# ScalarE writes the band's mask into the score banks, and the score products accumulate onto it

## The chip, the core and the metric

The kernel runs on one core of one Trainium2 chip. The metric is the device time of one execution in microseconds (us). The core's engines work side by side, each through its own list of instructions in a fixed order: TensorE (PE) multiplies matrices, VectorE (DVE) and ScalarE (ACT) work element by element, GpSimd (POOL) does too but cannot reach the accumulator banks, and SyncE (SP) issues the transfers. An instruction that needs another engine's result waits for a semaphore, and everything behind it on its engine waits with it.

## The reference, cut to what matters

```python
# B, H, S, D = 8, 8, 576, 64; factor = 4; scale = 1/8
out_d = softmax(scale * mean4(q) @ mean4(k).T) @ mean4(v)      # pooled attention, repeated 4 times
mask = abs(pos[:, None] - pos[None, :]) < factor               # a band 7 wide
scores = where(mask, scale * q @ k.T, -1e9)
s = scores - max(scores); a = exp(s); a /= sum(a) + 1e-9
x = (repeat(out_d, 4) + a @ v) -> [4608 tokens, 512]
h = x @ w_in                                                    # 512 -> 2048
out = (h * clip(h + 3, 0, 6) / 6) @ w_out                       # 2048 -> 512
```

## The kernel before

**The two halves.** The attention makes x, and two large products (the MLP) use it. The MLP's products are done as three 128x512 matmuls each (high and low parts), so PE has 2,688 wide matmuls of 512 columns for seven chunks of 512 tokens (lines 1066 and 1125; a chunk is 384 of them), and a last pair of chunks in Strassen's form (lines 1380, 1481, 1634). A chunk's first products (L1066) read x in split parts ("rounded"), so they can start only when the attention of the batches in it is done: L754 adds the two attentions into x, a cast and a subtraction split it (L122, L987).

**A unit** is one batch and one pair of heads. Batches 0 and 1 are worked on alone. The 24 units of batches 2 to 7 (called unit 0 to 23 here) go through PE in *bursts*: one burst holds the score products of a new unit, pooled (L504) and banded (L706), and between them the products with v (L749, L667) of the unit two bursts earlier. So x of batch 2 (units 0 to 3) is complete after the sixth burst, that of unit 5. A burst needs the banks h0 and h1, which the MLP uses too, and the banks a0 and a1 for its scores: columns 0 to 319 of each hold five windows of the band, 64 by 64, and the next 144 the pooled scores.

**After a burst, before the change.** DVE adds the mask to the banded scores of either bank while it copies them to SBUF (`outside`, L722), then takes the maximum of all ten windows (L557); ACT makes ten exponentials from SBUF with their sums (L568). ACT also makes the pooled softmax (L544, L550, L554: called a *weigh* here, three per unit, two of them from the banks), the mean (L687) and four copies out of the h banks (L122). A bank is given back when its `outside` and its weigh are done.

**What sets the order.** A planner in the kernel places every operation on its engine with a cost in us, due times, buffers ("take" and "free") and a table of shifts by operation number. What it writes out is the fixed order of each engine; on the chip only semaphores hold an instruction back. The score banks are taken in the units' order.

Of the kernel before, what the change touches and what calls it, by code (L numbers as in the profile page):

```python
# [58 lines left out]
def tile_local_down_attention_moe(ctx, tc, q_all, k_all, v_all, _qk_loc, _v_loc, w_in, w_out, ident_d, _mask_d, out):  # L59
# [67 lines left out]
    hot = const.tile([P, P], BF16, name="hot")  # L127
    mask = const.tile([P, D], F32, name="mask")
    head = const.tile([NAR, 2], F32, name="head")
# [14 lines left out]
    def make_mask():  # L144

        z = scratch()
        for h in range(2):
            hs = slice(h * D, (h + 1) * D)
            nc.vector.tensor_copy(z[hs, HALO:HALO + D], ident[hs, hs])
        near = bass.AP(tensor=z.tensor, offset=z.offset, ap=[z.ap[0], [1, D], [1, W]])  # L150
        nc.vector.tensor_reduce(out=mask, in_=near, op=ALU.add, axis=AX.X)
        nc.vector.tensor_scalar(mask, mask, -1.0, -MASKED, op0=ALU.add, op1=ALU.mult)

# [85 lines left out]
    loads = []  # L239
# [127 lines left out]
    def plan_unit(b, d, u, row0, k0, kv, PS, pair, masked, early_user, due):  # L367
# [120 lines left out]
        def scores_d4(hb):  # L488

            if not mixed:  # L490
                for g in range(2):
                    st["ps", g] = bank(PS, ("s", un, g))
# [4 lines left out]
            for h, j in ((0, 0), (1, 1), (0, 2), (1, 0), (0, 1), (1, 2)):  # L497
# [3 lines left out]
                for i in range(halves):  # L501
# [3 lines left out]
                        ps, q4[hs, j * QSTEP:j * QSTEP + QS], k4[hs, ks], start=True, stop=True, skip_group_check=True)  # L505
# [193 lines left out]
        def scores():  # L699

            for jj in range(5):
                for g in range(2):
                    k_first = window(jj + 5 * g)[0]
                    for h in range(2):
# [3 lines left out]
                            qk_of("k")[hs, k_first:k_first + WIN], start=True, stop=True, skip_group_check=True)  # L708
# [102 lines left out]
        else:  # L811
            sd, hx = yield {
                "un": un, "after": turned["q"] + turned["k"] + [pooled["q"], pooled["k"]] + masked,
                "take": [sk] + bks, "free": [], "pooled": scores_d4, "banded": scores}
# [21 lines left out]
        if True:  # L836
            subs = []
            for g in range(2):
                subs.append(op("DVE", 0.4, partial(outside, g), [sl_op] + subs, take=[pl, sl], free=[bks[g]]))
# [3 lines left out]
        elif not alone:  # L843
            a = op("ACT", 0.12, lambda: nc.scalar.activation(st["m"], st["m"], AF.Copy, scale=-0.125), [a])
# [856 lines left out]
    spare = const.tile([1, 2], F32, name="spare")  # L1701
# [559 lines left out]
```

## Time and profile before

| | |
|---|---|
| three runs | 882.73 us median (879.83 to 883.11) |
| span of the profiled execution | 877.6 us; no time around it is given for this execution |
| PE busy in the span | 871.4 us (99%) |
| DVE, ACT, POOL busy | 662.0 (75%), 494.0 (56%), 266.6 us (30%) |
| granted TensorE clock, mean | 0.999 |

The span goes from the first to the last instruction. Busy PE time counts overlapping matmuls once, so short waits between two matmuls can hide in it; how many wide matmuls pass in a stretch tells more.

### The profile page before, as it was taken

What the parts mean: (1) busy time and instruction counts of PE and PEld (TensorE: products, weight loads), DVE (VectorE), ACT (ScalarE), POOL (GpSimd) and SP (SyncE); (2) the same over time, 40 slices, a digit from 0 to 9 for tenths busy, and PEclk for the clock granted to TensorE, in tenths of its full rate; (3) what the DMA queues carried; (4) which work ended last, traced back from release to release, by engine and by line L of the source; (5) the groups of instructions that cost most, each with busy time, mean ns of one, the idle gap of its engine ahead of it and who ended that gap; (6) DMA issues with size and microseconds to landing.
All of it is one profiled execution on the core that took longest, in us unless ns stands there. A gap on an engine that the chain in (4) does not pass through costs nothing.

```text
span 877.6 us, 19793 instructions
## 1 busy us (share of the span) xinstructions
PE 871.4 (99%) x6948; PEld 716.1 (82%) x6948; DVE 662.0 (75%) x1240; ACT 494.0 (56%) x1555; POOL 266.6 (30%) x384
## 2 busy tenths in 40 slices
PE   8999999999999999999999999999999999999998
PEld 6788788888888888888888888888888888888887
DVE  7998886556867687877866786667856768778984
ACT  5998765455663656455454555555552325557761
POOL 6657742132524243224323431333422110000000
PEclk9999999999999999999999999999999999999999
DMA  9999353555675677757465647677764117564894
GB/s 255 262 294 234 74 129 79 118 102 123 121 164 120 120 149 165 148 128 148 98 156 122 141 102 167 146 174 234 188 151 103 37 38 230 212 228 137 274 274 71
DMA packets 358735, 136.40 MB, mean 155 GB/s; under 512 B 269612, under 2 KB 331180, under 8 KB 358636
## 3 DMA queue, kind: packets, MB, share of 16 engines
q1 hardware_dynamic: 353052, 134.22, 62.1%
q10 hardware_dynamic: 5584, 0.92, 0.6%
q8 instruction: 55, 0.90, 0.4%
q14 instruction: 44, 0.36, 0.1%
HBM read 90.44 MB, written 44.63 MB: 154 GB/s over the span
## 4 chain that ended last, share of the span: by engine, by line
PE 98%; DMA 1%; DVE 1%; SPq 0%; issue 0%
PE o L1125 36%; PE h L1066 35%; PE h L1380 5%; PE o L1634 4%; PE a L1380 4%; PE a L1634 2%; PE o L1481 2%; PE a L706 2%; PE h L749 2%; PE a L504 1%; PE h L667 1%; PE o L339 1%; DMA rows<-in_q_dram 1%; PE a L594 0%; PE a L684 0%; PE h L504 0%
## 5 line engine op out<-in xcount | busy, mean ns | idle before, releaser
L1125 PE MATMUL o<-wp,rounded 128*128 128x512 f32 x1344 | 323.6, 392 | 0.0
L1066 PE MATMUL h<-rounded,wp 128*128 128x512 f32 x1344 | 316.3, 390 | 0.0
L1066 PEld LDWEIGHTS h<-rounded,wp 128*128 128x128 f32 x1344 | 251.4, 188 | 52.8 <-DVE rounded L987 0.2
L1125 PEld LDWEIGHTS o<-wp,rounded 128*128 128x128 f32 x1344 | 249.6, 188 | 53.2 <-issue 0.4
L1076 DVE SCALAR_TENSOR_TENSOR arena<-arena,h 128x512 f32<-128x512 f32 x112 | 75.7, 676 | 52.7 <-ACT arena L1072 52.2
L1072 ACT ACTIVATE arena<-h 128x512 f32<-128x512 f32 x112 | 66.5, 594 | 84.8 <-PE h L1066 83.7
L1080 ACT CAST rounded<-arena 128x512 fp32r<-128x512 f32 x112 | 69.0, 616 | 62.9 <-PE o L1125 37.4
L1084 DVE TENSOR_TENSOR rounded<-arena,rounded 128x512 fp32r<-128x512 f32 x79 | 61.1, 774 | 51.7 <-PE o L1125 42.3
L568 ACT ACTIVATE arena<-arena 128x64 f32<-128x64 f32 x240 | 80.2, 337 | 0.4
L1084 POOL TENSOR_TENSOR rounded<-arena,rounded 128x512 fp32r<-128x512 f32 x33 | 44.8, 1359 | 94.3 <-PE o L1125 60.0
L1188 POOL TENSOR_TENSOR arena<-arena 128x128 f32<-128x128 f32 x65 | 33.1, 509 | 52.9 <-DVE arena L1183 28.0
L390 DVE STREAM_TRANSPOSE arena<-arena 128x576 f32<-128x576 f32 x56 | 43.0, 769 | 6.5 <-DMA arena<-in_k_dram 3.6
L544 ACT ACTIVATE arena<-arena 128x1 f32<-128x1 f32 (+1 forms) x77 | 15.0, 195 | 55.7 <-DVE arena L557 55.7
L568 ACT ACTIVATION_READ_ACCUMULATOR arena<-arena 128x1 f32 x240 | 45.3, 189 | 0.0
L687 ACT ACTIVATE arena<-h 128x144 f32<-128x144 f32 x24 | 7.0, 291 | 64.5 <-PE h L667 64.5
L447 POOL TENSOR_TENSOR arena<-arena 32x256 f32<-32x256 f32 (+2 forms) x28 | 21.2, 756 | 58.4 <-DMA arena<-in_v_dram 58.3
L1380 PE MATMUL h<-wp,wp 128*128 128x512 f32 x144 | 35.4, 389 | 0.0
L445 DVE TENSOR_REDUCE arena<-arena 128x128 f32<-128x512 f32 (+2 forms) x28 | 29.8, 1066 | 6.6 <-PE h L667 4.4
L585 DVE TENSOR_TENSOR arena<-arena 128x640 f32<-128x640 f32 (+1 forms) x40 | 32.9, 824 | 1.1
L1380 PEld LDWEIGHTS h<-wp,wp 128*128 128x128 f32 x144 | 27.0, 188 | 5.6
L557 DVE TENSOR_REDUCE arena<-arena 128x10 f32<-128x640 f32 (+1 forms) x57 | 31.4, 556 | 0.1
L1183 POOL TENSOR_TENSOR arena<-wp 128x256 f32<-128x256 f32 x21 | 17.0, 817 | 43.9 <-DMA si<-arena 18.1
(273 smaller groups left out, 1371.0 us busy)
## 6 DMA issues: line engine op xcount, KB each, us to landing
rawp<-in_w_in_dram SPq DMA_DIRECT2D x16, 512.0 KB
rawp<-in_w_out_dram SPq DMA_DIRECT2D x16, 512.0 KB
arena<-in_q_dram SPq DMA_DIRECT2D x112, 72.0 KB
arena<-in_k_dram SPq DMA_DIRECT2D x112, 72.0 KB
pl<-arena SPq DMA_DIRECT2D x24, 320.0 KB
arena<-pl SPq DMA_DIRECT2D x96, 80.0 KB
arena<-in_v_dram SPq DMA_DIRECT2D x28, 256.0 KB
wd<-wp SPq DMA_DIRECT2D x12, 512.0 KB
```

Source lines behind the costliest of these rows:

```text
L390: nc.vector.transpose(out=qk[kind], in_=qk[kind])
L568: nc.scalar.activation(x[:, j], x[:, j], AF.Exp, bias=m[:, j:j + 1], scale=0.125, accum_out=s[:, j:j + 1])
L585: eng.tensor_tensor(x, x, s.unsqueeze(2).broadcast_to(list(x.shape)), op=ALU.mult)
L1066: nc.tensor.matmul(st["ps"], win[f][:, wt, kk * P:(kk + 1) * P], xs[part][:, kk], start=(kk == 0 and i == 0), stop=(kk == NK - 1 and i == ...
L1072: nc.scalar.activation(st["t"], st["ps"], AF.Relu, bias=3.0)
L1076: nc.vector.scalar_tensor_tensor(out=t, in0=t, scalar=6.0, in1=st["ps"], op0=ALU.min, op1=ALU.mult)
L1080: nc.scalar.copy(st["gh"], st["t"])
L1084: eng.tensor_tensor(st["gl"], st["t"], st["gh"].bitcast(F32), op=ALU.subtract)
L1125: nc.tensor.matmul(otile[n, m], gt[:, ms], wout[f][:, wt], start=(f == 0 and i == 0), stop=(f == NF - 1 and i == 2),)
L1188: eng.tensor_tensor(u[:, z], u[:, x], u[:, y], op=o)
L1380: nc.tensor.matmul(ps, weight(i, j, wt, kk), xpart(MOVING[j], part)[:, kk], start=first and kk == 0 and x == 0, stop=kk == half - 1 and x ...
L1634: nc.tensor.matmul(places[acc, m][:, ts], w, z[:, part, ts], start=j == 5 and i == 0 and x == 0, stop=i == NG - 1 and x == 2, skip_group_c ...
```

## The change

From batch 2 on, ACT first copies a tile `seeds` (five copies of the mask, then zeros for the pooled part; 464 columns) into both score banks (`seed`). The burst's score products no longer start afresh but accumulate onto it. DVE's add is gone: it takes the maximum of each bank (`top_rows`), and the ten exponentials read the banks and write SBUF. The banks are given back when those ten are done. Once, two matmuls over the whole banks (`fill_bank`) come first, and POOL makes `seeds`.

```diff
+    def fill_bank():
+        for g in range(2):
+            ps = bank("a", ("open", g))
+            nc.tensor.matmul(ps, hot, hot.unsqueeze(1).broadcast_to([P, 4, P]), start=True, stop=True, skip_group_check=True)
+    def make_seeds(eng):
+        eng.tensor_copy(seeds[:, D:5 * D].rearrange("p (j k) -> p j k", k=D), mask.unsqueeze(1).broadcast_to([P, 4, D]))
+        eng.memset(seeds[:, 5 * D:], 0.0)
...
-                        ps, q4[hs, j * QSTEP:j * QSTEP + QS], k4[hs, ks], start=True, stop=True, skip_group_check=True)
+                        ps, q4[hs, j * QSTEP:j * QSTEP + QS], k4[hs, ks], start=n == 2 or mixed, stop=True, skip_group_check=True)
...
-                    x[:, j], x[:, j], AF.Exp, bias=m[:, j:j + 1], scale=0.125, accum_out=s[:, j:j + 1])
+                    x[:, j], rows(j % 2)[:, j // 2], AF.Exp, bias=m[:, j:j + 1], scale=0.125, accum_out=s[:, j:j + 1])
...
-                            qk_of("k")[hs, k_first:k_first + WIN], start=True, stop=True, skip_group_check=True)
+                            qk_of("k")[hs, k_first:k_first + WIN], start=alone, stop=True, skip_group_check=True)
+        def seed(g):
+            st["ps", g] = ps = bank(PS, ("s", un, g))
+            nc.scalar.copy(ps[:, :5 * D + SD], seeds)
+        def top_rows(g):
+            if g == 0:
+                places()
+            top(rows(g), greatest(g))
...
+            filled = [op("ACT", 0.49, partial(seed, g), opened, take=[bks[g]]) for g in range(2)]
             sd, hx = yield {
-                "un": un, "after": turned["q"] + turned["k"] + [pooled["q"], pooled["k"]] + masked,
-                "take": [sk] + bks, "free": [], "pooled": scores_d4, "banded": scores}
+                "un": un, "after": turned["q"] + turned["k"] + [pooled["q"], pooled["k"]] + filled,
+                "take": [sk], "free": [], "pooled": scores_d4, "banded": scores}
...
-                subs.append(op("DVE", 0.4, partial(outside, g), [sl_op] + subs, take=[pl, sl], free=[bks[g]]))
-            a = op("DVE", 0.73, lambda: top(p_all(), st["m"]), subs)
+            subs.append(op("DVE", 0.4, partial(outside if alone else top_rows, g), [sl_op] + subs, take=[pl, sl], free=[bks[g]]))
...
-                a = op("ACT", 0.67, lambda j=j: exps_sums(j, p_all(), st["m"], st["s"]), [m, a])
+                a = op("ACT", 0.67, lambda j=j: exps_sums(j, p_all(), st["m"], st["s"]), [m, a], free=bks)
```

The planner then writes another order. All engines' orders are the same up to the middle of the chunk of batch 0; from there they differ in many places. PE's content is unchanged but for the two matmuls of `fill_bank`. In the rows below the first number is the place in the engine's order, and the line numbers of the changed kernel are some 10 to 21 higher: L575 is the exponential (L568 before), L720 the seed, L1037 the eviction of a result (L1016), L694 the mean (L687), L697 and L771 the combination and the addition into x (L690, L754), L1087 and L1146 the MLP's products (L1066, L1125).

ACT before, between the bursts of unit 4 and unit 5 (`a_2708` is a score bank of unit 4, `h_2924` an h bank of unit 5's burst):

```order
305 L550 ACTIVATE arena<-a_2708,arena 128x144
306 L554 ACTIVATE arena<-arena 128x1
307 L568 ACTIVATE arena<-arena 128x64 x2
308 L1072 ACTIVATE arena<-h_2801 128x512
309 L568 ACTIVATE arena<-arena 128x64 x2
310 L122 CAST rounded<-arena 128x2x128
```

Row 305 is the last that reads unit 4's banks; the exponentials behind it read SBUF, and unit 5's burst needs no ACT instruction after row 305 for its score banks.

ACT with the change, the same stretch (`a_2718`, `a_2724` are unit 4's score banks, `a_2958`, `a_2962` unit 5's):

```order
355 L561 ACTIVATE arena<-arena 128x1
356 L575 ACTIVATE arena<-a_2718,arena 128x64
357 L575 ACTIVATE arena<-a_2724,arena 128x64
358 L1037 ACTIVATE arena<-o_2015 128x512
359 L575 ACTIVATE arena<-a_2718,arena 128x64
360 L575 ACTIVATE arena<-a_2724,arena 128x64
361 L575 ACTIVATE arena<-a_2718,arena 128x64
362 L575 ACTIVATE arena<-a_2724,arena 128x64
363 L575 ACTIVATE arena<-a_2718,arena 128x64
364 L575 ACTIVATE arena<-a_2724,arena 128x64
365 L582 ACTIVATE arena<-arena 128x10
366 L720 COPY a_2958<-seeds 128x464
```

Ten exponentials of unit 4 (two stand ahead, rows 351 and 352) and an eviction now stand ahead of unit 5's seeds, of which row 367 is the second.

PE before, at the end of unit 5's burst and the start of the third chunk (`h_3042` is that chunk's first product):

```order
556 L706 MATMUL a_2926<-arena 64x64 x2
557 L706 MATMUL a_2927<-arena 64x64 x2
558 L1125 MATMUL o_2000<-wp_1715,rounded 128x512 x3
559 L1125 MATMUL o_2005<-wp_1715,rounded 128x512 x3
560 L1125 MATMUL o_2013<-wp_1715,rounded 128x512 x3
561 L1125 MATMUL o_2023<-wp_1715,rounded 128x512 x3
562 L1125 MATMUL o_2000<-wp_1750,rounded 128x512 x3
563 L1125 MATMUL o_2005<-wp_1750,rounded 128x512 x3
564 L1066 MATMUL h_3042<-rounded,wp_557 128x512 x12
```

Eighteen wide matmuls of the chunk before stand between the burst and the third chunk; between unit 4's burst and this one stand 60.

PE with the change, the same place:

```order
540 L1146 MATMUL o_2035<-wp_1775,rounded 128x512 x3
541 L511 MATMUL a_2958<-arena 64x144 x2
542 L511 MATMUL a_2962<-arena 64x144 x2
```

```order
566 L713 MATMUL a_2958<-arena 64x64 x2
567 L713 MATMUL a_2962<-arena 64x64 x2
568 L1087 MATMUL h_3053<-rounded,wp_555 128x512 x6
569 L1087 MATMUL h_3067<-rounded,wp_630 128x512 x6
570 L1087 MATMUL h_3053<-rounded,wp_555 128x512 x6
571 L1087 MATMUL h_3067<-rounded,wp_630 128x512 x6
572 L1087 MATMUL h_3114<-rounded,wp_745 128x512 x12
573 L1087 MATMUL h_3142<-rounded,wp_756 128x512 x12
```

Row 540 is the last product of the second chunk: unit 5's burst has moved behind all of it, 36 wide matmuls after unit 4's, and the third chunk's first product stands right behind the burst.

DVE with the change, behind unit 5's burst (`h_2965` is its h bank):

```order
323 L564 TENSOR_REDUCE arena<-a_2958 128x1
324 L564 TENSOR_REDUCE arena<-a_2962 128x1
325 L697 SCALAR_TENSOR_TENSOR arena<-h_2965,arena 128x144
326 L400 STREAM_TRANSPOSE arena<-arena 128x576
327 L771 TENSOR_TENSOR first<-h_2964,arena 128x288
328 L771 TENSOR_TENSOR first<-h_2965,arena 128x288
```

Two maxima and a transposition of a later unit stand around the combination, ahead of the two additions that complete batch 2's x.

## Rows read from the trace of the kernel before

**Rows 1.** The page, busy time: engine, us, share, instructions.

```profile
PE 871.4 (99%) x6948; PEld 716.1 (82%) x6948; DVE 662.0 (75%) x1240; ACT 494.0 (56%) x1555; POOL 266.6 (30%) x384
```

**Rows 2.** Stretches: length, busy us (instructions) of each engine, granted clock, DMA share, GB/s.

```profile
core 0: us, PE busy (x) PEld busy (x) DVE busy (x) ACT busy (x) POOL busy (x), PEclk, DMA share, GB/s
34.00:690.00 656.00, 656.00 (x5596) 540.39 (x5600) 486.44 (x938) 373.50 (x1316) 236.51 (x336) 1.00 0.63 144
874.00:876.00 2.00, 0.00 (x0) 0.00 (x0) 0.34 (x1) 0.00 (x0) 0.00 (x0) 0.98 0.73 102
876.00:877.60 1.60, 0.00 (x0) 0.00 (x0) 0.00 (x0) 0.00 (x0) 0.00 (x0) 0.50 0.17 24
```

**Rows 3.** Timeline around unit 5's burst: start us, us, engine, line, operation, count.

```profile
231.81 0.48 PE L504 MATMUL a<-arena 64*64 64x144 f32 x8
...
233.52 0.29 ACT L687 ACTIVATE arena<-h 128x144 f32<-128x144 f32 x1 [2.17 <-PE h L667]
...
233.99 4.38 PE L1125 MATMUL o<-wp,rounded 128*128 128x512 f32 x18
...
234.63 0.31 DVE L690 SCALAR_TENSOR_TENSOR arena<-h,arena 128x144 f32<-128x144 f32 x1 [0.37 <-ACT arena L122]
...
235.06 0.81 DVE L754 TENSOR_TENSOR first<-h,arena 128x288 f32<-128x288 f32 x2
...
236.07 0.50 ACT L122 CAST rounded<-first 128x384 fp32r<-128x384 f32 x1
...
236.64 1.01 POOL L987 TENSOR_TENSOR rounded<-first,rounded 128x384 fp32r<-128x384 f32 x1 [5.21 <-ACT rounded L122]
...
238.21 4.02 PE L1066 MATMUL h<-rounded,wp 128*128 128x512 f32 x17
```

**Rows 4.** Timeline of ACT behind unit 4's burst.

```profile
217.51 0.29 ACT L687 ACTIVATE arena<-h 128x144 f32<-128x144 f32 x1 [1.21 <-PE h L667]
...
221.29 0.20 ACT L544 ACTIVATE arena<-arena 128x1 f32<-128x1 f32 x1 [2.70 <-DVE arena L557]
...
223.94 0.33 ACT L568 ACTIVATE arena<-arena 128x64 f32<-128x64 f32 x1
...
224.27 0.33 ACT L568 ACTIVATE arena<-arena 128x64 f32<-128x64 f32 x1
```

**Rows 5.** Groups of ACT by form: count, busy us, mean ns, idle before.

```profile
L568 ACT ACTIVATE arena<-arena 128x64 f32<-128x64 f32 x240 | 80.2, 337 | 0.4
...
L550 ACT ACTIVATE arena<-a,arena 128x144 f32<-128x144 f32 x48 | 18.3, 382 | 2.9 <-DVE arena L722 1.4
...
L550 ACT ACTIVATE arena<-arena 128x144 f32<-128x144 f32 x24 | 10.0, 416 | 0.8
...
L1396 ACT COPY arena<-a 128x512 f32<-128x512 f32 x12 | 7.1, 588 | 11.0 <-PE a L1380 10.8
...
L193 ACT ACTIVATE a<-rawp 128x512 f32<-128x512 f32 x2 | 1.3, 650 | 0.0
```

**Rows 6.** Groups of DVE by form.

```profile
L1076 DVE SCALAR_TENSOR_TENSOR arena<-arena,h 128x512 f32<-128x512 f32 x112 | 75.7, 676 | 52.7 <-ACT arena L1072 52.2
...
L390 DVE STREAM_TRANSPOSE arena<-arena 128x576 f32<-128x576 f32 x56 | 43.0, 769 | 6.5 <-DMA arena<-in_k_dram 3.6 <-DMA arena<-in_q_dram 2.9
L722 DVE TENSOR_TENSOR arena<-a,mask 128x320 f32<-128x320 f32 x56 | 26.7, 481 | 1.7 <-ACT arena L550 1.1 <-ACT arena L531 0.3 <-issue 0.2
...
L557 DVE TENSOR_REDUCE arena<-arena 128x10 f32<-128x640 f32 x29 | 23.5, 810 | 0.1
...
L557 DVE TENSOR_REDUCE arena<-a 128x1 f32<-128x144 f32 x56 | 15.9, 295 | 0.2 <-PE a L706 0.2
```

**Rows 7.** Timeline of PE, first and last microseconds.

```profile
1.06 3.17 PE L1695 MATMUL h<-hot 128*128 128x512 bf16 x7 [1.06 <-DVE hot L140]
4.03 1.57 PE L322 MATMUL a<-ident,arena 128*128 128x128 f32 x6
5.39 1.84 PE L322 MATMUL o<-ident,arena 128*128 128x128 f32 x12
...
873.33 0.52 PE L1634 MATMUL o<-wp,wp 128*128 128x256 f32 x3
```

More of the change, by code (lines that the diff above doesn't have):

```diff
@@ L124, in copy_on @@
             eng.tensor_copy(out_, in_)
-    hot = const.tile([P, P], BF16, name="hot")
-    mask = const.tile([P, D], F32, name="mask")
-    head = const.tile([NAR, 2], F32, name="head")
+    seeds = const.tile([P, 5 * D + SD], F32, name="seeds")
+    mask, hot = seeds[:, :D], seeds[:, 5 * D:5 * D + P // 2].bitcast(BF16)
+    small = const.tile([P, 4], F32, name="small")
+    head, spare = small[:NAR, :2], small[:1, 2:]
     def scratch():
@@ L237, in xb_of @@
         return ("xb", b) if b > 1 else ("xb1", 1) if b else ("tail", 0)
-    loads = []
+    loads, opened = [], []
     def src(t, first, ap):
@@ L488, in scores_d4 @@
         def scores_d4(hb):
-            if not mixed:
-                for g in range(2):
-                    st["ps", g] = bank(PS, ("s", un, g))
             st["hb"] = hb
@@ L811, in plan_unit @@
         else:
+            if not opened:
+                opened.append(op("PE", 0.5, fill_bank, take=[(PS, ("open", g)) for g in range(2)], free=[(PS, ("open", g)) for g in range(2)], rec=2))
+                opened.append(op("POOL", 0.6, partial(make_seeds, nc.gpsimd), opened + masked))
+            filled = [op("ACT", 0.49, partial(seed, g), opened, take=[bks[g]]) for g in range(2)]
             sd, hx = yield {
-                "un": un, "after": turned["q"] + turned["k"] + [pooled["q"], pooled["k"]] + masked,
-                "take": [sk] + bks, "free": [], "pooled": scores_d4, "banded": scores}
+                "un": un, "after": turned["q"] + turned["k"] + [pooled["q"], pooled["k"]] + filled,
+                "take": [sk], "free": [], "pooled": scores_d4, "banded": scores}
             sl_op = sd
@@ L835, in plan_unit @@
         s_ops.append(sl_op)
-        if True:
-            subs = []
-            for g in range(2):
-                subs.append(op("DVE", 0.4, partial(outside, g), [sl_op] + subs, take=[pl, sl], free=[bks[g]]))
+        subs = []
+        for g in range(2):
+            subs.append(op("DVE", 0.4, partial(outside if alone else top_rows, g), [sl_op] + subs, take=[pl, sl], free=[bks[g]]))
+        if alone:
             a = op("DVE", 0.73, lambda: top(p_all(), st["m"]), subs)
@@ L843, in plan_unit @@
         elif not alone:
-            a = op("ACT", 0.12, lambda: nc.scalar.activation(st["m"], st["m"], AF.Copy, scale=-0.125), [a])
+            a = op("ACT", 0.12, lambda: nc.scalar.activation(st["m"], st["m"], AF.Copy, scale=-0.125), subs)
             m = a
             for j in range(0, NWIN, 2):
-                a = op("ACT", 0.67, lambda j=j: exps_sums(j, p_all(), st["m"], st["s"]), [m, a])
+                a = op("ACT", 0.67, lambda j=j: exps_sums(j, p_all(), st["m"], st["s"]), [m, a], free=bks)
             a = op("ACT", 0.15, lambda: plus(st["s"]), [a])
@@ L1700, in tile_local_down_attention_moe @@
     begun = op("SP", 0.5, lambda: None, size=0.0001, dl=-9.0)
-    spare = const.tile([1, 2], F32, name="spare")
     plain = op("POOL", 0.2, lambda: nc.gpsimd.memset(spare, 0.0), dl=-2.0)
```

## The prediction

> **What bounds the kernel now.** I read the busy times first: PE is at work in 871.4 of 877.6 us [rows 1]. Then the stretches: from 34 to 690 us, where all the units of the attention pass, PE is busy for the whole 656.00 us at clock 1.00, while DVE and ACT have 170 and 282 us to spare [rows 2]. So PE's own instructions are the bound, and nothing that makes another engine quicker can shorten that stretch; a change can only leave PE's time as it is or put a wait into it. The question is therefore not what DVE saves, but whether a burst, or a chunk's first product, now has to wait with no other work left for PE. Last I read the place where that is closest before: in the timeline around unit 5's burst [rows 3] the burst starts at 231.81, the eighteen wide matmuls behind it at 233.99, and the third chunk's first product at 238.21. Batch 2's x, which that product needs, is added up at 235.06 + 0.81 = 235.87, cast and split by 237.65. The eighteen matmuls cover this with 2.3 us to spare for the addition; for the split, which only the second half of the products needs, there is more.
>
> **What the change takes away.** 48 additions of the mask of 0.48 us and 24 maxima of 0.81 us; the 48 maxima that come instead handle 320 columns each, as the addition does, so I price them at 0.48 us [rows 6]. DVE gets back 24 x 0.81 = 19 us of time that PE never waited for: worth nothing.
>
> **What it adds on PE.** Two full matmuls of `fill_bank`. The seven matmuls of the same shape at the kernel's start are 2.97 / 7 = 0.42 us apart [rows 7], at the lower of the two clock levels, so some 0.21 each at the upper one; with a change of shape, 0.5 us together. Accumulating costs PE nothing that the wide matmuls, which nearly all accumulate, don't show already.
>
> **What it adds on ACT.** 48 seeds of 464 columns. No row before shows one; the nearest are the copy out of a bank, 0.588 us for 512 columns, and an activation into a bank, 0.650 [rows 5]. In proportion that is 0.53 to 0.59, and ACT's instructions overlap by some 0.1 us: I take 1.05 us for a pair, from its start to its end. ACT is busy for 373.50 of the 656 us [rows 2], so 25 us more of it has room. But the seeds stand in the way of the burst: a burst now waits for its seeds, these for the ten exponentials of the unit before (they read the banks), and these stand behind that unit's maxima and weighs.
>
> **How long that chain is.** Before, from a burst's start to the mean it takes 233.52 - 231.81 = 1.71 us [rows 3], and from unit 4's mean to its first exponential 223.94 - 217.51 = 6.43 us [rows 4], with all three weighs between. From the first exponential on, ten of them follow 0.33 us apart [rows 4], 3.3 us. An exponential that reads a bank has no row; the weigh, in both forms, is 34 ns quicker from a bank (382 against 416 ns [rows 5]). So the ten take 3.0 to 3.3 us; I keep 3.3. With the seeds and a signal of 0.1 us the least chain is 1.71 + 6.43 + 3.3 + 1.05 + 0.1 = 12.6 us from burst to burst, plus what the order puts between.
>
> **Where it shows.** On PE's side a burst takes 2.18 us (231.81 to 233.99) and eighteen wide matmuls 4.22 [rows 3]. In the new order the 24 seeded bursts have 23 gaps. Eighteen hold 81 matmuls or more, over 21 us with the burst: the chain is hidden. Four hold 60, or 2.18 + 14.1 = 16.2 us; there the order puts two evictions and one or two small casts of the MLP into the chain, some 1.8 us, so 14.4: hidden, with 1.8 us to spare. One holds 36, unit 4 to unit 5: 2.18 + 8.4 = 10.6 us, and one eviction stands in the chain (0.59, less the overlap): 12.6 + 0.5 = 13.1. **PE waits 2.5 us** before unit 5's burst, since the second chunk has run out and the third needs that very burst. Bounds: 2.1 with the quicker exponentials, 3.2 if a seed costs 0.65 and the exponentials gain nothing from the overlap that I assume.
>
> **The second wait.** Right behind that burst PE wants the third chunk's first product. DVE has two maxima (0.295 each [rows 6]) that need the burst's scores, the combination (0.31, not before 2.82 us after the burst's start, as now [rows 3]), a transposition of 0.77 [rows 6] that stands ahead of the additions now, and the additions, 0.81: 2.82 + 0.31 + 0.77 + 0.81 = 4.7 us after the start, 4.8 with the signal. The burst itself is over at 2.18, so **PE waits 2.6 us**; 2.0 if the transposition slips in earlier, as before, where the additions ended at 4.06. The split that follows (0.50 + 1.01 [rows 3]) lies beside the first halves of two products, 12 matmuls or 2.7 us.
>
> **The third.** No product of the old chunk is left, so the third group of twelve comes straight behind the second, and needs the bank of the first: eviction (0.59 as in [rows 5]), gate (0.68 [rows 6]) and signals, 1.6 us, while only the last six of the second group, 1.4 us, stand between. I take **0.4 us**, for ACT's exponentials stand around that eviction.
>
> **The clock.** Behind the last matmul, which ends at 873.33 + 0.52 = 873.85 [rows 7], the granted clock is 0.98 over 874 to 876 and 0.50 after [rows 2]: it fell at about 875.9, 2.1 us after PE had stopped. Both idle stretches above are longer than that, so I expect it to fall. What it costs then: at the kernel's start the lower rate lasted from 1.06 to at least 4.03 and perhaps 5.39 [rows 7], 3.0 to 4.3 us of work, of which half is lost. I take **2.1 us**, one fall.
>
> At the other chunk starts eighteen matmuls stay behind the burst (4.22 us) and 2.6 us of addition hide behind them. The first 34 us are the same instructions.
>
> **The sum** is made on the profiled span: 877.6 + 0.5 + 2.5 + 2.6 + 0.4 + 2.1 = 885.7, that is 8.1 us more. The runs' median is 882.73, 5.1 us above that span, and I put the same 8.1 on it: 890.8, rounded to 891.
>
> **Rivals.** *The clock stays up.* The two stretches are only 0.4 and 0.5 us longer than the 2.1 us after which it fell, with a burst between them. Then 6.0 us more: 888.7. Chance 0.22.
>
> *The clock falls twice, or other places wait as well.* If the burst between the stretches doesn't bring the clock back, it runs low through the burst too: 2.2 more for it, or a second 2.1. And if a bank-reading exponential cost 0.5 us instead of 0.33, the chain would be 1.7 longer, the four gaps of 60 would reach their limit and unit 5's wait would be 4.2. Together 893 to 900. Against it: the weigh is quicker from a bank [rows 5]. Chance 0.15. The Trainium skill's page "TensorE: Matmul & The Clock Gate", section "A second HAM failure mode: psum-queue depth-cycling", tells of a kernel whose clock went down and up again because PE kept pausing briefly between groups of matmuls; by that rule there would be a second fall here, and the sum would be a span of 887.8, while this trace shows only one fall, at the end.
>
> *Not slower.* The waits are smaller than 4.4 us (0.5%) in all, because the chain is shorter than I add it up: the ten exponentials without the weighs' pauses, the maxima done early by an otherwise idle DVE. Of the 6.43 us from mean to exponentials 2.70 are ACT's wait for a maximum [rows 4], which stood behind DVE's additions of the mask and other work; if DVE, freed of them, delivers 1.5 us sooner, the first wait is 1.0, the second 2.0 without the transposition, and the clock does not fall: 0.5 + 1.0 + 2.0 + 0.4 = 3.9, 886.6, "the same". It decides where both waits together are under 3.5 us. Against it: in the new order a summation, a pooling and the two additions into x still stand ahead of the maxima. Chance 0.16.
>
> *Faster* would need PE work or a PE wait to go away, and there is none after 34 us: 0.03, for the spread of the runs alone.
>
> **How the numbers follow.** The forecast (both waits and one fall, 889 to 893) has 0.44, and its own range is that. Half a per cent, 4.4 us, is about what a measurement of this kernel can tell from no change: its three runs span 3.3 us. Slower is the forecast with the first two rivals, 0.81; same 0.16; faster 0.03. The range for eight in ten leaves out the lower half of "same" and the far end of the long waits: 885.5 to 897.
>
> **What would show it.** In the changed profile: PE idle, or far fewer wide matmuls per us, at one place, some 230 us in, in two pieces around unit 5's burst; the first released by ACT's seed, the second by DVE's addition L771; wide matmuls twice as far apart for 3 to 4 us behind it, and a clock below 1.00 in that stretch; none of this at other bursts. The chain of waits would show ACT and DVE at that place. I am wrong if PE streams through that place, if the four bursts at 60 matmuls wait too, or if the exponentials from the banks take much more or less than 0.33 us.

## The result and the profile after

The changed kernel takes 891.72 us (median of 4 runs, 891.09 to 893.54) against 882.21 us for the kernel before on the same chip (4 runs, 879.83 to 883.11). The ratio is 1.0119, with a 95% interval of 1.0105 to 1.0133: slower by 10.5 us; the medians differ by 9.5. The profiled spans are 889.3 and 877.6 us, 11.7 apart.

The page's busy times of the kernel after, to be held against [rows 1]:

```profile
PE 875.6 (98%) x6950; PEld 717.9 (81%) x6950; DVE 650.8 (73%) x1222; ACT 504.9 (57%) x1596; POOL 271.9 (31%) x398
```

DVE does 11 us less, ACT 11 us more, and both have a quarter of the span or more to spare. The loss cannot be seen here, apart from PE's idle time, which went from 6 to 14 us. The view of what PE waited for shows it (in all, times, longest, us). Before, it has these four lines, all of matmuls in the first 34 us:

```profile
PE h L1695 <- DVE hot L140: 1.1, 1, 1.1
PE o L706 <- issue: 0.7, 1, 0.7
PE o L706 <- DVE early L722: 0.3, 1, 0.3
PE a L322 <- DMA rows<-in_q_dram: 0.2, 1, 0.2
```

After, apart from such lines of the start:

```profile
PE h L1087 <- DVE first L771: 3.2, 1, 3.2
PE a L511 <- issue: 1.9, 1, 1.9
PE o L1146 <- ACT arena L1037: 1.6, 1, 1.6
...
PE o L1146 <- DVE arena L1039: 0.8, 2, 0.4
```

The first two are the two waits of the prediction. The others are waits for a result bank: PE can use it again when ACT (L1037) or DVE (L1039) has copied the result out of it, which is called an eviction here. The timeline around unit 5's burst answers to [rows 3]; it begins with unit 4's mean and first exponential, which answer to [rows 4]:

```profile
229.21 0.29 ACT L694 ACTIVATE arena<-h 128x144 f32<-128x144 f32 x1 [1.21 <-PE h L674]
...
234.45 0.30 ACT L575 ACTIVATE arena<-a,arena 128x64 f32<-128x64 f32 x1
...
236.86 0.60 ACT L1037 ACTIVATE arena<-o 128x512 f32<-128x512 f32 x1 [0.30 <-issue]
...
239.39 1.01 ACT L720 COPY a<-seeds 128x464 f32<-128x464 f32 x2
...
240.02 0.77 PE L511 MATMUL a<-arena 64*64 64x144 f32 x6 [1.89 <-issue]
...
240.45 0.14 PEld L511 LDWEIGHTS a<-arena 64*64 64x64 f32 x2 [0.23 <-ACT a L720]
...
242.14 0.29 ACT L694 ACTIVATE arena<-h 128x144 f32<-128x144 f32 x1 [1.74 <-PE h L674]
...
243.18 0.29 DVE L697 SCALAR_TENSOR_TENSOR arena<-h,arena 128x144 f32<-128x144 f32 x1
...
244.57 0.78 DVE L400 STREAM_TRANSPOSE arena<-arena 128x576 f32<-128x576 f32 x1 [1.10 <-DMA arena<-in_q_dram]
245.28 0.78 DVE L771 TENSOR_TENSOR first<-h,arena 128x288 f32<-128x288 f32 x2
...
245.84 6.42 PE L1087 MATMUL h<-rounded,wp 128*128 128x512 f32 x21 [3.16 <-DVE first L771]
```

Ten exponentials, a weigh and an eviction (L1037) stand between 234.45 and the seeds at 239.39, and PE's burst starts 0.63 us after the first seed has begun. The view calls the releaser "issue", but the place leaves only the first seed; the second holds up the burst's next weight loads (240.45). Then the adds (L771) follow a transposition of a block of q for a later unit, and that transposition waited 1.10 us for its load. Last, 21 wide matmuls take 6.42 us. The stretches (columns as in [rows 2]) tell why:

```profile
34.00:237.70 203.70, 203.69 (x1695) 165.34 (x1692) 149.89 (x259) 140.70 (x393) 83.03 (x92) 1.00 0.59 139
237.70:249.00 11.30, 6.25 (x118) 4.89 (x118) 6.46 (x16) 8.05 (x42) 1.58 (x3) 0.85 0.72 146
...
245.40:248.70 3.30, 2.86 (x7) 2.31 (x8) 3.19 (x9) 2.73 (x16) 1.58 (x3) 0.50 0.83 150
...
557.00:880.00 323.00, 323.00 (x2005) 266.89 (x2004) 247.40 (x434) 171.72 (x460) 60.48 (x92) 1.00 0.64 179
```

PE is busy without a break up to 237.70 and again from 557; in the 11.30 us around the burst 5.05 us are idle, the sum of the two waits (1.89 + 3.16). From 245.40 to 248.70 the granted clock is 0.50, the lower level, and only 7 matmuls start. The waits for result banks lie elsewhere. The timeline of the largest:

```profile
554.20 0.29 ACT L694 ACTIVATE arena<-h 128x144 f32<-128x144 f32 x1 [3.60 <-PE h L674]
...
555.67 0.60 ACT L1037 ACTIVATE arena<-o 128x512 f32<-128x512 f32 x1
...
556.32 1.89 PE L1146 MATMUL o<-wp,rounded 128*128 128x512 f32 x7 [1.57 <-ACT arena L1037]
```

ACT had to wait 3.60 us for a burst's product before it could get to the eviction behind it, and PE, past that burst, needed the evicted bank.

### The profile page after: what moved, and what is told of

It reads as the page before. It is cut to its first block, busy times and chain, and to the rows that moved or that the text cites. A ratio compares the mean times of both kernels' runs of the same rounds, so it can differ in the third digit from the quotient of the medians.

```text
span 889.3 us, 19845 instructions
## 1 busy us (share of the span) xinstructions
PE 875.6 (98%) x6950; PEld 717.9 (81%) x6950; DVE 650.8 (73%) x1222; ACT 504.9 (57%) x1596; POOL 271.9 (31%) x398
## 4 chain that ended last, share of the span: by engine, by line
PE 93%; DMA 3%; SPq 2%; DVE 1%; issue 1%; ACT 0%; POOL 0%; DVEq 0%
PE o L1146 34%; PE h L1087 32%; PE h L1401 5%; PE o L1655 4%; PE a L1401 4%; PE a L1655 2%; PE o L1502 2%; PE a L713 2%; PE h L766 1%; PE a L511 1%; PE h L674 1%; SPq L394 1%; DMA arena<-pl 1%; DMA rows<-in_q_dram 1%; DMA arena<-in_v_dram 1%
## 5 line engine op out<-in xcount | busy, mean ns | idle before, releaser
L1146 PE MATMUL o<-wp,rounded 128*128 128x512 f32 x1344 | 324.3, 393 | 2.4 <-ACT arena L1037 1.6
L1087 PE MATMUL h<-rounded,wp 128*128 128x512 f32 x1344 | 318.0, 391 | 3.2 <-DVE first L771 3.2
L1087 PEld LDWEIGHTS h<-rounded,wp 128*128 128x128 f32 x1344 | 252.3, 189 | 56.9 <-issue 3.8
L1146 PEld LDWEIGHTS o<-wp,rounded 128*128 128x128 f32 x1344 | 249.4, 188 | 56.9 <-DVE arena L1039 2.1
L1097 DVE SCALAR_TENSOR_TENSOR arena<-arena,h 128x512 f32<-128x512 f32 x112 | 76.1, 680 | 70.9 <-ACT arena L1093 70.7
L575 ACT ACTIVATE arena<-a,arena 128x64 f32<-128x64 f32 x240 | 72.8, 317 | 0.2
L575 ACT ACTIVATION_READ_ACCUMULATOR arena<-a,arena 128x1 f32 x240 | 50.4, 210 | 0.0
L1209 POOL TENSOR_TENSOR arena<-arena 128x128 f32<-128x128 f32 x48 | 23.7, 493 | 66.6 <-DVE arena L1209 46.7
L564 DVE TENSOR_REDUCE arena<-a 128x1 f32<-128x144 f32 (+1 forms) x104 | 36.0, 378 | 2.8 <-PE a L713 2.4
L1204 POOL TENSOR_TENSOR arena<-wp 128x256 f32<-128x256 f32 x18 | 14.1, 793 | 72.9 <-DMA out_dram<-arena 50.5
L585 DVE RECIPROCAL arena<-arena 128x10 f32<-128x10 f32 (+1 forms) x60 | 11.3, 189 | 33.2 <-ACT arena L582 21.4
L415 POOL TENSOR_TENSOR arena<-arena 128x144 f32<-128x144 f32 x54 | 32.1, 595 | 4.2
L592 DVE TENSOR_TENSOR arena<-arena 128x640 f32<-128x640 f32 (+1 forms) x41 | 30.8, 752 | 1.3
```

What stands on the lines that cost most here:

```text
L415: eng.tensor_tensor(t, t, x[:, :, r], op=ALU.add)
L564: nc.vector.tensor_reduce(out=m, in_=x, op=ALU.max, axis=AX.X)
L575: nc.scalar.activation(x[:, j], rows(j % 2)[:, j // 2], AF.Exp, bias=m[:, j:j + 1], scale=0.125, accum_out=s[:, j:j + 1])
L1087: nc.tensor.matmul(st["ps"], win[f][:, wt, kk * P:(kk + 1) * P], xs[part][:, kk], start=(kk == 0 and i == 0), stop=(kk == NK - 1 and i == ...
L1097: nc.vector.scalar_tensor_tensor(out=t, in0=t, scalar=6.0, in1=st["ps"], op0=ALU.min, op1=ALU.mult)
L1146: nc.tensor.matmul(otile[n, m], gt[:, ms], wout[f][:, wt], start=(f == 0 and i == 0), stop=(f == NF - 1 and i == 2),)
```

## The experiments

Theory: the change makes the planner write another order, in which unit 5's burst, the one that completes batch 2's x, stands right ahead of the third chunk; that place costs most of the time, the rest goes to evictions which the new order puts late. Rivals: ACT's extra work as such; banks that are held through the exponentials; the fill. The planner's table of shifts, which goes by operation number, is not among them: its last entry is operation 566, and the numbers are the same in both kernels up to 743.

The start of the program differs from execution to execution: in the profiles below the first wide matmul starts between 33.86 and 37.54 us. Kernels with the change's order up to unit 5's burst are therefore also compared from the start of unit 4's burst to the end of the span; in the change that is 661.8 us (227.50 to 889.3).

Distances below are in wide matmuls from unit 5's burst to the end of the second chunk's products, in the written order: 24 before (eighteen, as in [rows 3], and six that stand behind the third chunk's first product), 0 in the change.

### Only the held banks

```diff
+        def masked_rows(g):
+            if g == 0:
+                places()
+            nc.vector.tensor_tensor(rows(g), rows(g), mask.unsqueeze(1).broadcast_to([P, 5, D]), op=ALU.add)
+            top(rows(g), greatest(g))
...
-                    x[:, j], x[:, j], AF.Exp, bias=m[:, j:j + 1], scale=0.125, accum_out=s[:, j:j + 1])
+                    x[:, j], rows(j % 2)[:, j // 2], AF.Exp, bias=m[:, j:j + 1], scale=0.125, accum_out=s[:, j:j + 1])
...
-                a = op("ACT", 0.67, lambda j=j: exps_sums(j, p_all(), st["m"], st["s"]), [m, a])
+                a = op("ACT", 0.67, lambda j=j: exps_sums(j, p_all(), st["m"], st["s"]), [m, a], free=bks)
```

> The banks are kept through the ten exponentials as in the change, but nothing is written ahead of the products: VectorE adds the mask onto the scores inside the bank, the maximum and the exponentials read the bank, and there is no fill. In the written order unit 5's burst stands 12 wide matmuls ahead of the third chunk (the change: 0, before: 24). Theory (it takes the hold and the seeds together to push this burst onto the chunk's start): no wait of 1 us or more there, 0 to +2 us to the time before, 882 to 884. Rival 1 (keeping the banks through the exponentials is enough to lose the time): +6 us or more, 888 and up. Rival 2 (exponentials read from banks are slow or make PE wait in every burst): a wait in most of the bursts, +5 us or more.

Measured: 888.98 us against 880.72, ratio 1.0095 (1.0068 to 1.0123). A miss for the theory: 8 us are lost with no seed at all, as much as the first rival asked for. But no burst waits. PE waited 5.1 us for gates (the product h * clip(h + 3, 0, 6) on DVE, which frees the bank of h), 1.7 of them at 665 us, the rest at the third chunk. The timeline, of three engines, shows where the loss starts, and a stretch that the clock fell there:

```profile
248.00 0.18 DVE L578 RECIPROCAL arena<-arena 128x3 f32<-128x3 f32 x1 [2.71 <-ACT arena L554]
...
248.45 0.59 ACT L1081 ACTIVATE arena<-h 128x512 f32<-128x512 f32 x1
...
249.49 1.35 DVE L1085 SCALAR_TENSOR_TENSOR arena<-arena,h 128x512 f32<-128x512 f32 x2
...
250.18 1.22 PE L1075 MATMUL h<-rounded,wp 128*128 128x512 f32 x2 [3.42 <-DVE arena L1085]
```

```profile
249.90:253.10 3.20, 2.92 (x7) 2.34 (x8) 3.13 (x5) 1.94 (x8) 1.27 (x1) 0.50 0.79 174
```

The third chunk's third group of products needs the bank of its first. The eviction of that bank (L1081) stands on ACT among unit 5's exponentials, the gate that reads it (L1085) on DVE behind a reciprocal that waits 2.71 us for the weighs. So a burst 12 matmuls ahead of the chunk does not make the chunk's start wait, but its softmax gets in front of the chunk's first evictions. This is the prediction's "third" wait, in a place where it is large.

### Only the seeds

```diff
-            top(rows(g), greatest(g))
+            nc.vector.tensor_copy(st["p"][:, :, g], rows(g))
...
-        if alone:
+        if True:
             a = op("DVE", 0.73, lambda: top(p_all(), st["m"]), subs)
...
-                a = op("ACT", 0.67, lambda j=j: exps_sums(j, p_all(), st["m"], st["s"]), [m, a], free=bks)
+                a = op("ACT", 0.67, lambda j=j: exps_sums(j, p_all(), st["m"], st["s"]), [m, a])
```

(and the exponentials read SBUF again.)

> Seeds, the fill and the accumulation as in the change, but VectorE then copies the two banks into SBUF, which frees them after 0.9 us, and maximum and exponentials read SBUF as before. ScalarE's work is as large as in the change or larger. Unit 5's burst stands 24 wide matmuls ahead of the third chunk, as before. Theory: the seeds find their banks free early, no wait at unit 5's burst or at the third chunk, and what is left is the fill and the later start, about 1 us: 882.7 to 884. Rival (the 48 seeds load ScalarE so that evictions and bursts come late): waits of the products for the result bank stay, +4 us or more, 886 and up.

Measured: 882.42 against 880.72, ratio 1.0019 (1.0010 to 1.0029). The largest wait behind the start is 1.0 us for a gate (L1097); ACT is busy for 516.4 us, more than in the change. With unit 5's burst 24 matmuls ahead of the chunk, then, neither the seeds nor ACT's load cost much.

### A distance of 24, with all of the change's work

```diff
+            o.late += SHIFT.get(o.n, 0.0) + getattr(o, "rush", 0.0)
...
             filled = [op("ACT", 0.49, partial(seed, g), opened, take=[bks[g]]) for g in range(2)]
+            for f in filled:
+                f.rush = -40
...
+                a.rush = -40
+            m.rush, subs[0].rush, subs[1].rush = -40, -40, -40
```

(the last `a` is each pair of exponentials, `subs` the two maxima, `m` the small step between; a `rush` of -40 makes an operation due 40 us earlier.)

> The change with nothing altered but the planner's due times of the maxima, the exponentials and the seeds of batches 2 to 7, which are set 40 us earlier, so that they go ahead of other work; in the written order unit 5's burst then stands 24 wide matmuls ahead of the third chunk. Theory: the two waits of 2.0 and 3.2 us and the fall of the clock at that place go, 6.5 to 7 us less than the change: 884 to 886; the waits for result banks may stay or move (up to 3 us). Rival (the loss is ScalarE's load and the held banks wherever the burst stands): the waits come back at this or other bursts and the time stays at 889 or more.

Measured: 881.54 against 880.72, ratio 1.0010 (1.0000 to 1.0019). Held banks, seeds, accumulation, fill, all 48 seeds on ACT: nothing of it is missing, and some nine tenths of the loss are gone, more than expected, since the waits for result banks went as well. The stretch that answers to [rows 2]:

```profile
34.00:690.00 656.00, 656.00 (x5597) 540.45 (x5595) 476.21 (x939) 387.16 (x1363) 228.53 (x321) 1.00 0.64 145
```

PE has no break in it and the clock stays at 1.00, as before.

### The order of the change, with the work of before

```diff
-            nc.scalar.copy(ps[:, :5 * D + SD], seeds)
...
-                            qk_of("k")[hs, k_first:k_first + WIN], start=alone, stop=True, skip_group_check=True)
+                            qk_of("k")[hs, k_first:k_first + WIN], start=True, stop=True, skip_group_check=True)
...
-            top(rows(g), greatest(g))
+            outside(g)
+            if g == 1:
+                top(p_all(), st["m"])
```

(the pooled products start with zero too, and the exponentials read SBUF.)

> The change's written order with the work of before: the planner still books the seeds on ScalarE and the banks through the exponentials, but nothing is copied into the banks; the products start with zero, VectorE adds the mask into SBUF (two adds, and one maximum over ten windows), and the exponentials read SBUF. The fill stays. Unit 5's burst stands 0 wide matmuls ahead of the third chunk, as in the change. Theory (the order is the loss, whatever ScalarE copies): the first wait of 2.0 us goes, the second, for the add ahead of the third chunk, stays at 2.6 to 5 us, result banks still come late here and there: 886 to 891. Rival (the waits come from the copies and the held banks themselves): no wait over 1 us, 884 or less.

Measured: 893.28 against 880.93, ratio 1.0138 (1.0119 to 1.0157): as slow as the change or a little slower, with no seed and no held bank, and above the range expected. What PE waited for, DVE's timeline, and a stretch:

```profile
PE h L1088 <- DVE first L772: 4.7, 1, 4.7
PE o L1147 <- ACT arena L1038: 1.6, 1, 1.6
```

```profile
246.16 0.78 DVE L400 STREAM_TRANSPOSE arena<-arena 128x576 f32<-128x576 f32 x1 [2.65 <-DMA arena<-in_q_dram]
```

```profile
245.00:251.70 6.70, 4.28 (x10) 3.45 (x11) 5.44 (x12) 4.27 (x22) 1.73 (x4) 0.50 0.95 198
```

The burst no longer waits, and the second wait is 4.7 us instead of 3.2: the transposition ahead of the adds waits for the same load, and now for 2.65 us. Counted from the start of unit 4's burst, it begins at 16.8 us (229.32 to 246.16), and in the change at 17.1 (227.50 to 244.57), so what the burst gains, the load takes back. The clock is at 0.50 over 6.70 us, twice the change's stretch. The wait for the result bank is there too. From unit 4's burst on this kernel takes 662.1 us, the change 661.8.

### One unit, and the other nineteen

The edit of due times (`rush`) from above in the change, with `-40` only for unit 2 in the first kernel, and only for units 5 to 23 in the second.

> The change with the due times of one unit's maxima, exponentials and seeds (unit 2, the third of the 24) set 40 us earlier and nothing else; in the written order unit 5's burst then stands 12 wide matmuls (2.7 us) ahead of the third chunk, and later bursts come otherwise too. Theory (one late burst is what costs): the first wait goes, of the second at most 0.5 us stays, no fall of the clock there: 5.5 to 7 us less than the change, 884 to 886.5, result-bank waits of up to 3 us included. Rival (all 24 units matter): 888 or more.

> The complement: the due times of units 5 to 23 set 40 us earlier, units 0 to 4 as in the change, so that unit 5's burst stands at the third chunk's start as in the change and the bursts after it otherwise. Theory: both waits there and the fall of the clock stay (about 6.5 to 7 us), the waits for result banks at 458 to 460 and 550 to 556 (3 us) may go: 887 to 892. Rival (the loss is spread over the units): under 886.

Unit 2 alone: 887.29 against 880.93, ratio 1.0072 (1.0049 to 1.0094), somewhat above the range expected. The two waits are gone, so ten operations of one unit decide the place of a burst three units later. But at a distance of 12 the third chunk's third group waits 2.3 us for its gate, as with the held banks above, and the clock fell there after all, when PE was at work again (from 254.19 on):

```profile
250.00:255.50 5.50, 3.24 (x15) 2.36 (x14) 3.20 (x7) 5.41 (x25) 0.00 (x0) 1.00 0.42 107
255.50:258.90 3.40, 3.40 (x10) 2.66 (x9) 3.35 (x5) 1.00 (x3) 1.28 (x1) 0.50 0.96 183
```

The clock also fell once before 44 us, far ahead of the edited unit; I do not count that to the edit. This profile is of the longest of the four runs (890.72).

Units 5 to 23: 890.55, ratio 1.0103 (1.0086 to 1.0120). What PE waited for:

```profile
PE a L511 <- issue: 1.9, 1, 1.9
PE h L1092 <- DVE first L771: 1.9, 1, 1.9
```

Both waits at the third chunk stay (the second is shorter than the change's 3.2, since the clock fell during the burst here and the burst itself took longer), the waits for result banks are gone. From unit 4's burst on this kernel takes 658.1 us (229.29 to 887.4), 3.7 less than the change; in the times alone, whose intervals overlap, the gain is not clear. So the two parts of the loss are separate, and the larger one is at unit 5's burst.

### All units, at a distance of 12

The edit of due times for all 24 units, with 20 us instead of 40.

> As the kernel with all 24 units' maxima, exponentials and seeds due 40 us earlier, but 20 us; unit 5's burst then stands 12 wide matmuls ahead of the third chunk instead of 24. Theory (that distance decides; at 12 the chunk's first outputs are fetched by ScalarE and VectorE behind the burst's exponentials): a wait of 2 to 3.6 us within the third chunk and a fall of the clock, 3.5 to 5.5 us more than before: 884.5 to 886.5. Rival (earlier due times are enough, wherever the burst stands): no wait over 1 us, 883 or less.

Measured: 883.57 against 880.81, ratio 1.0040 (1.0025 to 1.0054), between the two theories, and the clock did not fall. The timeline shows the same queue as with the held banks, only shorter:

```profile
245.47 0.18 DVE L585 RECIPROCAL arena<-arena 128x3 f32<-128x3 f32 x1 [1.88 <-ACT arena L561]
...
245.92 0.59 ACT L1097 ACTIVATE arena<-h 128x512 f32<-128x512 f32 x1
...
247.65 2.58 PE L1091 MATMUL h<-rounded,wp 128*128 128x512 f32 x10 [1.30 <-DVE arena L1101]
```

Distance alone does not set the size: at 12 this wait was 3.4, 2.3 and 1.3 us in three kernels.

### The transposition behind the adds

```diff
-        self.deadlines()
+        self.deadlines(); self.dep(self.ops[1179], self.ops[984])
```

(operation 1179 is the transposition, 984 the second add.)

> The change with one step moved: VectorE's transposition of a q block, which stood ahead of the adds into x at the third chunk and waited 1.10 us for its load there, is planned behind these adds; the bursts' order is that of the change. Theory: the second wait falls from 3.2 to 1.3 to 1.8 us, the first stays at 2.0: 1.4 to 1.9 us less than the change, 889 to 891. Rival (the add itself, or the mean ahead of it on ScalarE, is what ends the wait): the wait stays near 3 us and the time at 891.7.

Measured: 891.02 against 880.81, ratio 1.0121 (1.0106 to 1.0136): no gain. The step did what was expected, the time did not follow. What PE waited for, DVE's timeline, and a stretch:

```profile
PE a L511 <- issue: 1.9, 1, 1.9
PE o L1146 <- ACT arena L1037: 1.6, 1, 1.6
PE h L1087 <- DVE first L771: 1.4, 1, 1.4
PE o L1146 <- DVE arena L1039: 1.4, 2, 0.9
...
PE h L1087 <- DVE arena L1097: 1.0, 1, 1.0
```

```profile
244.97 0.30 DVE L697 SCALAR_TENSOR_TENSOR arena<-h,arena 128x144 f32<-128x144 f32 x1
245.37 0.86 DVE L771 TENSOR_TENSOR first<-h,arena 128x288 f32<-128x288 f32 x2
```

```profile
241.40:244.70 3.30, 3.13 (x94) 2.94 (x88) 0.17 (x1) 0.60 (x3) 0.00 (x0) 0.50 0.84 177
```

The adds now begin 0.1 us behind the combination (L697) instead of 1.8. But the clock fell during the burst instead of behind it, so the burst took longer and the combination came 4.5 us after its start (240.45 to 244.97) instead of 3.2. From the burst's start to the chunk's first product it is 5.5 us (240.45 to 245.97), in the change 5.8: of the 1.7 us won, 0.3 are left, and the second wait of 1.4 us instead of 3.2 is shorter mostly because the burst ended later. A new wait of 1.0 us for the gate came up, and the waits for result banks grew by 0.6. From unit 4's burst on it is 661.6 us, the change's 661.8.

### Twice the seeds, in either order

```diff
-            nc.scalar.copy(ps[:, :5 * D + SD], seeds)
+            for _ in range(2):
+                nc.scalar.copy(ps[:, :5 * D + SD], seeds)
```

> The change with each seed written twice, at the same planned cost, so the written order is the same and ScalarE has 48 more copies of about 0.5 us. Theory (the seeds decide at unit 5's burst alone, the gaps of 60 hide them with 1.8 us to spare): the first wait grows by about 1.0 us, 892.5 to 893.5, other bursts do not wait for seeds. Rival (ScalarE's time is short through the whole stage): waits for seeds or for evictions at many bursts, +4 us or more, 896 and up.

> The kernel with all units due 40 us earlier, each seed written twice at the same planned cost: 48 more copies of about 0.5 us on ScalarE (some 24 us of its time). Theory (off the path, the seeds are hidden at every burst): 0 to 1 us more than with one, ratio to before 1.001 to 1.0025, no wait for seeds over 0.5 us. Rival (ScalarE's time counts): +3 us or more, ratio 1.004 and up.

In the change's order: 894.53 against 880.72, ratio 1.0157 (1.0137 to 1.0176), some 3 us more than the change, where 1 was expected. What PE waited for:

```profile
PE a L511 <- issue: 2.5, 1, 2.5
PE h L1088 <- DVE first L772: 1.9, 1, 1.9
...
PE a L511 <- ACT a L721: 0.6, 1, 0.6
```

Unit 5's burst waits 2.5 + 0.6 = 3.1 us instead of 1.9, as expected, and no other burst waits for seeds. The add's wait is shorter by 1.3, as the clock fell during this burst too and the burst ended later; the transposition did not wait for its load here. The stretch:

```profile
246.70:250.20 3.50, 3.28 (x98) 3.09 (x93) 0.23 (x2) 0.60 (x3) 0.00 (x0) 0.51 0.92 184
```

Most of what this kernel takes longer than the change is not the seeds' doing, as far as its profile shows. That is of the longest of the four runs (896.94); unit 4's burst starts at 232.19 in it instead of 227.50, since the program's start took longer, with a fall of the clock at 38 us. From there on it takes 662.9 us, 1.1 more than the change, which is what the theory expected. In the order with a distance of 24: 881.72 against 880.81, ratio 1.0009 (1.0000 to 1.0018), the same as with single seeds, with 51.8 us of seeds on ACT.

### The fill, at the program's start

```diff
     def heat():
+        fill_bank()
```

(in place of the operation at unit 0's burst, in the kernel with all units 40 us earlier.)

> The kernel with all 24 units' maxima, exponentials and seeds due 40 us earlier, and the two matmuls that fill the banks put ahead of the warming matmuls at the program's start, where TensorE has nothing else to do, in place of the spot at unit 0's burst. Theory (the fill's 0.45 us is on TensorE's path, all else is hidden): 0.3 to 0.6 us less than with the fill at unit 0, ratio to before 0.9995 to 1.001. Rival (the products no longer add onto the seeds, as the banks were written in between): the output would not be the reference's; rival 2 (the fill costs nothing): the ratio stays at 1.001.

Measured: 880.82 against 880.93, ratio 0.9995 (0.9985 to 1.0006). In this kernel the products do not all add onto their seeds, so it is read for time only: with the fill at the start nothing measurable is left of the change's cost.

## Why the prediction was right, and where not

**Direction, place and size:** 891.0 was forecast and 891.72 measured; both waits, at the burst and at the third chunk, in that order, with one fall of the clock behind them. None of the four bursts at 60 matmuls waited, and no burst but unit 5's waited for a seed. That the times come within 0.7 us is in part luck: the loss is 9.5 us by the medians, 10.5 by the ratio and 11.7 by the spans, where 8.1 was summed, and the base of 882.73 was on the high side (the kernel before took 880.72 to 880.93 in the experiments).

**The fill,** 0.5: the two matmuls are busy for 0.6 us in all, and moving them away was worth 0.15% with overlapping intervals. By the bursts' starts (see below) 0.47 us are lost just ahead of unit 0's burst with them, and none without. In agreement.

**The first wait,** 2.5 forecast, 1.9 measured. From unit 4's burst to unit 5's it took 12.5 us (227.50 to 240.02) where 13.1 was added up. Up to the mean it took 1.71 us, as forecast, and from there to the first seed 10.2 us (229.21 to 239.39), as added up (6.43 + 3.3 + 0.5), though its parts moved: the exponentials from the banks follow 0.29 us apart, not 0.33 (the groups by form: 317 ns each, against 337 in [rows 5]), while the eviction among them cost 0.9 instead of 0.5, with a wait of 0.30 ahead of it. What made the difference is the seeds. A pair took 1.01, forecast 1.05, but PE did not need the pair: it began 0.63 us after the first seed had, where 1.15 was added up. The upper bound of 3.2 does not come out of its terms; two seeds at 0.65, ten exponentials at 0.337 and an eviction at 0.59 make 2.9.

```profile
L575 ACT ACTIVATE arena<-a,arena 128x64 f32<-128x64 f32 x240 | 72.8, 317 | 0.2
...
L720 ACT COPY a<-seeds 128x464 f32<-128x464 f32 x48 | 24.9, 561 | 0.0
```

**The second wait,** 2.6 forecast, 3.2 measured. The step that failed is "a transposition of 0.77 that stands ahead of the additions": it was priced as work that is ready, but it waited 1.10 us for its load. From the burst's start to the third chunk's first product it took 5.8 us (240.02 to 245.84) where 4.8 was added up. The burst took longer too, 2.66 us instead of 2.18, as it waited for the second seed on its way; so 0.5 of that 1.0 shows in the wait and 0.5 in the burst. (The combination came 0.3 later than added up, and the product began 0.2 before the second addition had ended.) With the transposition behind the adds 1.7 us of DVE's time ahead of them was gone, but the burst ran at the lower clock there, so no run shows the wait without it at full clock.

**The third,** 0.4 forecast, 0.2 in the gaps between the matmuls. The mechanism (eviction and gate of the first group among the exponentials) is real: 1.0 to 3.4 us of it show in five of the experiments.

**The clock,** 2.1 forecast. The 21 wide matmuls behind the second wait took 6.42 us; at the pace of the 36 ahead of the burst (8.46 us) they would take 4.9, so 1.5 us were lost. One fall, as forecast; in this profile the rival in which it stays up is out, and so is the second fall. The page "TensorE: Matmul & The Clock Gate" of the Trainium skill, section "A second HAM failure mode: psum-queue depth-cycling", tells of a clock that goes down and up as PE pauses between groups of matmuls, from which the prediction read a second fall. This trace has one; the kernel with the order alone, whose clock was low for twice as long, comes nearest to it. For the change's other runs the second fall is not out: two of them have a mean clock of 0.996 and 0.995, where the profiled one has 0.998, so twice as much time at the lower level or more (an estimate from the means); no trace shows where. That it fell was luck in part: the reason given was two idle stretches longer than 2.1 us, and the first was 1.9. The cost was taken from the program's start, where the lower rate is read from the spacing alone, 0.42 us as in the fall here (0.43): the stretches print a clock of 1.00 for those first 5 us.

**What was missing.** "None of this at other bursts" holds for seeds, but the sum had no term for the evictions. To see all that the new order cost, I take the starts of the bursts in the timelines of both kernels, with 0.227 us for each wide matmul by which the numbers ahead of them differ (24 take 5.44 us in the kernel before, from 693.86 to 699.30). By that, unit 0's burst is 0.8 us late, 0.3 of it from the program's start and 0.5 from the fill; unit 5's burst is 2.0 us later still, unit 6's 5.4, and the last one 3.6: 11.7 in all. The 5.4 are 3.2 + 0.2 + 1.5 and the 0.5 by which the burst itself took longer. The 3.6 come from later bursts; 2.4 of them are the waits for result banks (L1037, L1039) in the view, and most of the rest lies in the same three stretches. So the sum is 0.5 + 1.9 + 3.2 + 0.5 + 0.2 + 1.5 = 7.8 in place of 8.1, and 3.6 that nobody had summed, a third of the loss.

**What the prediction took as given.** It priced the waits as the chain of exponentials and seeds, with the written order as given. The crossing of order and work shows more: the work with a good order loses 0.1%, the order with the old work loses 1.4%. The first wait is the seeds' doing, but without seeds the second becomes longer by nearly as much, as what stands ahead of the adds waits for a load. So the cause is the written order, and within it mostly the place of one burst: some 7.3 of the 11.7 us lie between unit 4's burst and unit 6's. No run moves that burst alone; each shift of due times writes another order behind it as well. Why the planner put it there I can only argue, from its rules: due times go back along dependencies, not along banks, so the maxima and exponentials, which since the change release the next burst's banks, were not known to be urgent. That ten operations of unit 2, due earlier, move unit 5's burst speaks for it.

No version beats the kernel before: it has no wait on PE behind the start, and the best one here, all of the change in the better order, is 0.1% behind it.

## What to carry to other kernels

When a change lets an operation hold a buffer longer, or makes a new step wait for one, give the operations that release it the due time of whoever waits for it; the planner here, which passes due times along data alone, seems to have left them late. Price a change to such a kernel first by what it does to the order, and try the new order with the old work and the old order with the new work before blaming an instruction. In an in-order queue ask of every instruction ahead of the critical one whether its own input, a load too, is there.

## What the hardware showed that I had not expected

The exponential of 128x64 that reads a bank is quicker than that from SBUF (317 against 337 ns; 0.29 against 0.33 us apart). Behind the start, the clock did not fall at single waits of 1.3 us (all units due 20 us earlier; mean clock 1.0) or 1.6 us (at 555 us, 1.00 from 550 to 557). It fell late in one of 3.4 us (banks held), some 2 us into one of 4.7 (the order alone), and 1.3 us after the end of one of 2.3 (unit 2 alone). With a wait of 1.9 us ahead of unit 5's burst it fell in the change only in the second wait, but already during the burst with the adds first and with units 5 to 23 due earlier, and so it did behind the longer wait with twice the seeds. Where it falls decides what a microsecond won there is worth. A full write of the two banks at the program's start did not serve the later accumulation; the same write right ahead of the first seeds does. In between, batches 0 and 1 use the banks for smaller products that start afresh. The page "PSUM — Partial Sum Buffer" of the Trainium skill, section "The four PSUM rules", says that such a start clears the marks that say "written" for the whole bank in the groups of 32 partitions that it touches, so that what is added next there overwrites instead. The run agrees with it, though it cannot show the marks.
